# Banded attention and a cosine-gated layer on one core: the layer's tiles are moved between the attention heads, matmuls without use are added, and the PSUM pools become one

## The chip, the cores and the metric

The kernel runs on one core of a Trainium2 chip. The core has five engines that work through queues of their own, in order: TensorE (PE; its weight loads are listed as PEld), VectorE (DVE), ScalarE (ACT), GpSimd (POOL) and SyncE (SP), which here issues all DMAs. They wait for each other by semaphores. The metric is the time of one execution on the device in microseconds (us).

## What is computed

Eight batches of eight heads, 576 positions, head width 64. A query sees a key if they lie within 32 positions or if one of the two is among 8 global positions. The result, 4608 rows of 512, goes through a layer of width 2048 whose gate is `h * cos(h)`:

```
scores = q @ k.T / sqrt(64)
mask   = (abs(pos_i - pos_j) <= 32) | is_global_i | is_global_j
attn   = softmax(where(mask, scores, -1e9)) @ v     # 8 x 8 heads, 576 x 64
x      = attn, heads side by side                   # 4608 x 512
h      = x @ w_in                                   # 4608 x 2048
out    = (h * cos(h)) @ w_out                       # 4608 x 512
```

## The kernel before

**Start.** The mask is built once for five key blocks (`mask_sb`, five blocks of up to 128 keys by 576 queries; POOL writes a block in line 93). Both weight matrices are loaded and cast to float16 on ScalarE (lines 105 and 109).

**Attention, 64 heads.** Per head SyncE loads q, k and v in six DMAs; VectorE casts q and k, POOL casts v, which has an extra column of ones, so that the sum of the weights comes out beside the result. TensorE transposes q and k in five blocks each (line 148, tile `pst`), ScalarE copies them to `qT` and `kT` (line 149). For each of the five key blocks there are two score matmuls, of 512 and 64 queries (line 157, tile `ps`), two exps on ScalarE (line 163, to `e_sb`), and one multiply by the mask on VectorE (line 166, to `pmt`). For each of the five query blocks five matmuls over the key blocks follow (PV, line 175, tile `po`), a reciprocal (line 182), a scaling to `attn16` (line 184) and a DMA to `x_dram` in device memory (line 187).

**The layer, 36 tiles of 128 rows**, after all heads. Per tile: load the rows (line 203), four transposes (line 207) with ScalarE copies (line 208); for each of 16 column blocks four matmuls (line 213, `ph`), a cosine as a shifted sine on ScalarE (line 218), a multiply on VectorE (line 219, `gT`); then 16 matmuls of 512 columns (line 222, another tile named `po`), a copy (line 226) and a store (line 227).

**What sets the order.** The code is unrolled. A scheduler takes the instructions by their place in the code and by when it reckons their inputs and a free buffer to be there, and writes one fixed list for each engine; on the chip each list runs in order. The pools' buffer counts decide how far one step can run ahead of the next: in attention four buffers for transposes, two for scores, two for PV, two for `e_sb`, `recip` and `attn16`; in the layer two, four (`ph`) and two.

Of the kernel before, what the change touches and what calls it, by code (L numbers as in the profile page):

```python
# [18 lines left out]
def kernel(  # L19
# [56 lines left out]
    for kb in range(NKB):  # L76
        kbs = KBS[kb]
        pst = ps_small.tile([P, P], FP32, tag="isgt_ps")
# [3 lines left out]
    mask_sb = mpool.tile([P, NKB, S], FP16)  # L82
    for kb in range(NKB):
        kbs = KBS[kb]
# [15 lines left out]
    w_in16 = wpool.tile([P, DM // P, DFF], FP16)  # L100
    w_out16 = wpool.tile([P, DFF // P, DM], FP16)
# [9 lines left out]
    x_dram = dram.tile([NT, DM], FP16)  # L111

    qkv_pool = ctx.enter_context(tc.tile_pool(name="qkv", bufs=3))
    es_attn = ExitStack()
    tpsum = es_attn.enter_context(tc.tile_pool(name="tpsum", bufs=4, space=bass.MemoryType.PSUM))
    spsum = es_attn.enter_context(tc.tile_pool(name="spsum", bufs=2, space=bass.MemoryType.PSUM))
    opsum = es_attn.enter_context(tc.tile_pool(name="opsum", bufs=2, space=bass.MemoryType.PSUM))
    work = ctx.enter_context(tc.tile_pool(name="work", bufs=2))

    for b in range(B):  # L120
        for h in range(H):
            q_f32 = qkv_pool.tile([P, NKB, D], FP32, tag="qf32")
            k_f32 = qkv_pool.tile([P, NKB, D], FP32, tag="kf32")
# [11 lines left out]
            for kb in range(NKB):  # L135
                kbs = KBS[kb]
# [7 lines left out]
            for eng, src, dst in ((nc.scalar.copy, q_sb, qT), (nc.scalar.copy, k_sb, kT)):  # L144
                for kb in range(NKB):
                    kbs = KBS[kb]
                    pst = tpsum.tile([D, P], FP16, tag="tr")
                    nc.tensor.transpose(pst[:, :kbs], src[:kbs, kb], ident16[:kbs, :kbs])  # L148
                    eng(dst[:, kb * P : kb * P + kbs], pst[:, :kbs])  # L149

            pmt = work.tile([P, NKB, S], FP16, tag="pmt")
            for kb in range(NKB):
                kbs = KBS[kb]
                e_sb = work.tile([P, S], FP16, tag="e")
                for c0, cn in ((0, 512), (512, S - 512)):
                    ps = spsum.tile([P, 512], FP32, tag="st")
                    nc.tensor.matmul(  # L157
                        ps[:kbs, :cn],
                        kT[:, kb * P : kb * P + kbs],
                        qT[:, c0 : c0 + cn],  # L160
                        start=True, stop=True,
                    )
                    nc.scalar.activation(  # L163
                        e_sb[:kbs, c0 : c0 + cn], ps[:kbs, :cn], AF.Exp, scale=scale
                    )
                nc.vector.tensor_tensor(  # L166
                    pmt[:kbs, kb], e_sb[:kbs, :], mask_sb[:kbs, kb], ALU.mult
                )

            for qb in range(NKB):  # L170
                qbs = KBS[qb]
                po = opsum.tile([P, D + 1], FP32, tag="pv")
                for kb in range(NKB):
                    kbs = KBS[kb]
                    nc.tensor.matmul(  # L175
                        po[:qbs, :],
                        pmt[:kbs, kb, qb * P : qb * P + qbs],
                        v_sb[:kbs, kb, :],
                        start=(kb == 0), stop=(kb == NKB - 1),
                    )  # L180
# [11 lines left out]
    es_attn.close()  # L192

    xpool = ctx.enter_context(tc.tile_pool(name="xpool", bufs=2))
    xtpsum = ctx.enter_context(tc.tile_pool(name="xtpsum", bufs=2, space=bass.MemoryType.PSUM))
    hpsum = ctx.enter_context(tc.tile_pool(name="hpsum", bufs=4, space=bass.MemoryType.PSUM))
    outpsum = ctx.enter_context(tc.tile_pool(name="outpsum", bufs=2, space=bass.MemoryType.PSUM))
    NTT = NT // P
    NF = DFF // P
    NC = DM // P  # L200
    for t in range(NTT):
        x_sb = xpool.tile([P, DM], FP16, tag="x")
        nc.sync.dma_start(x_sb, x_dram[t * P : (t + 1) * P, :])
        xT = xpool.tile([P, NC, P], FP16, tag="xT")
        for j in range(NC):
            pst = xtpsum.tile([P, P], FP16, tag="xtr")
            nc.tensor.transpose(pst, x_sb[:, j * P : (j + 1) * P], ident16)
            nc.scalar.copy(xT[:, j], pst)  # L208
        gT = xpool.tile([P, NF, P], FP16, tag="gT")
        for f in range(NF):  # L210
            ph = hpsum.tile([P, P], FP32, tag="hT")
            for j in range(NC):
                nc.tensor.matmul(  # L213
                    ph, w_in16[:, j, f * P : (f + 1) * P], xT[:, j],
                    start=(j == 0), stop=(j == NC - 1),
                )
            cos_sb = xpool.tile([P, P], FP16, tag="cos")
            nc.scalar.activation(cos_sb, ph, AF.Sin, bias=pio2)  # L218
            nc.vector.tensor_tensor(gT[:, f], cos_sb, ph, ALU.mult)  # L219
        po = outpsum.tile([P, DM], FP32, tag="out")  # L220
        for f in range(NF):
            nc.tensor.matmul(  # L222
                po, gT[:, f], w_out16[:, f], start=(f == 0), stop=(f == NF - 1)
            )
        o_sb = xpool.tile([P, DM], FP32, tag="osb")
        nc.scalar.copy(o_sb, po)  # L226
        nc.sync.dma_start(out[t * P : (t + 1) * P, :], o_sb)


# [28 lines left out]
```

## Time and profile before

| | |
|---|---|
| median of six runs | 947.8 us (945.39 to 949.38) |
| the profiled execution | 945.39 us |
| its span, first to last instruction | 943.6 us |
| TensorE busy | 767.6 us (81%) |
| ScalarE busy | 564.4 us (60%) |
| VectorE busy | 470.3 us (50%) |
| POOL busy | 121.5 us (13%) |

Busy shares here are means over two stages that differ: attention up to about 613 us, the layer after it. A busy TensorE in this table is not TensorE at its peak, since matmuls overlap and their ends are modelled. A duration of one instruction contains its latency; what a row of them needs is read from the distance of their starts. "Waiting for" in a row names what came last, by semaphores.

### The profile page before, as it was taken

Reading aid. Unit: us, or ns where it says so; the run is one execution under the profiler, and the core shown is the slowest. Engines: PE = TensorE matmul, PEld = TensorE weight load, DVE = VectorE, ACT = ScalarE, POOL = GpSimd, SP = SyncE. Lnnn points to the kernel's source line nnn. Section 1 sums busy time; section 2 is a strip of 40 time slices with the busy share of each in tenths; the row PEclk is TensorE's granted clock in tenths of the full one; section 3 lists DMA queues with packets and bytes.
Section 4 is the critical chain, followed back from the end, with each engine's and each line's share of the span. In section 5 each row is a group of like instructions: output and inputs, shape, how many; then the busy total and the mean of one; then the engine's idle time right before and its main releaser. Section 6 shows DMA issues by size and latency. Waiting matters only on the chain.

```text
span 943.6 us, 19000 instructions
## 1 busy us (share of the span) xinstructions
PE 767.6 (81%) x5913; PEld 433.2 (46%) x5913; DVE 470.3 (50%) x1820; ACT 564.4 (60%) x2046; POOL 121.5 (13%) x406
## 2 busy tenths in 40 slices
PE   1688787777787887878878878799889889898997
PEld 0243333333343433434333344376666666666664
DVE  4454545444555455555555554455545445454453
ACT  3765555555455565555546556566766667667675
POOL 6211212121112112121121211100000000000000
PEclk9999999999999999999999999999999999999999
DMA  9433233332222322322222211010111111111110
GB/s 352 99 65 66 64 67 71 65 68 53 58 57 53 65 53 53 66 60 53 59 60 59 57 37 22 20 40 31 52 51 35 52 36 51 52 35 51 43 44 34
DMA packets 171798, 56.84 MB, mean 60 GB/s; under 512 B 159920, under 2 KB 164528, under 8 KB 171184
## 3 DMA queue, kind: packets, MB, share of 16 engines
q1 hardware_dynamic: 171696, 55.62, 23.5%
q8 instruction: 46, 0.75, 0.3%
q14 instruction: 56, 0.46, 0.2%
HBM read 41.42 MB, written 14.16 MB: 59 GB/s over the span
## 4 chain that ended last, share of the span: by engine, by line
PE 50%; ACT 21%; DVE 13%; issue 7%; DMA 7%; POOL 2%; ACTq 0%; SPq 0%; DVEq 0%; POOLq 0%
PE ps L157 14%; PE po L175 12%; ACT e_sb L163 11%; PE po L222 10%; PE ph L213 7%; DMA x_dram<-attn 7%; ACT cos_sb L218 6%; PE pst L148 6%; DVE gT L219 4%; DVE pmt L166 4%; ACT xT L208 2%; DVE attn L184 2%; POOL mask_sb L93 1%; DVE recip L182 1%; ACT w_out L109 1%
## 5 line engine op out<-in xcount | busy, mean ns | idle before, releaser
L163 ACT ACTIVATE e_sb<-ps 128x512 f16<-128x512 f32 (+3 forms) x640 | 230.3, 406 | 252.3 <-DVE pmt L166 158.0
L157 PE MATMUL ps<-qT,kT 64*128 64x512 f16 (+3 forms) x640 | 214.6, 424 | 88.8 <-ACT e_sb L163 79.4
L219 DVE TENSOR_TENSOR gT<-cos_sb,ph 128x128 f16<-128x128 f16 x576 | 157.5, 288 | 163.3 <-ACT cos_sb L218 162.5
L218 ACT ACTIVATE cos_sb<-ph,pio 128x128 f16<-128x128 f32 x576 | 182.1, 367 | 45.2 <-DVE gT L219 34.3
L213 PE MATMUL ph<-xT,w_in 128*128 128x128 f16 x2304 | 182.2, 219 | 29.8 <-DVE gT L219 15.8
L175 PE MATMUL po<-v_sb,pmt 128*128 128x65 f16 (+3 forms) x1600 | 181.2, 241 | 25.5 <-DVE attn L184 22.9
L213 PEld LDWEIGHTS <-w_in 128*128 128x128 f16 x2304 | 154.1, 97 | 72.4 <-issue 62.7
L175 PEld LDWEIGHTS <-pmt 128*128 128x128 f16 (+3 forms) x1600 | 117.2, 124 | 143.5 <-DVE attn L184 57.4
L166 DVE TENSOR_TENSOR pmt<-e_sb,mask_sb 128x576 f16<-128x576 f16 (+1 forms) x320 | 144.7, 459 | 60.7 <-ACT e_sb L163 59.5
L222 PE MATMUL po<-w_out,gT 128*128 128x512 f16 x576 | 152.6, 379 | 0.0
L182 DVE RECIPROCAL recip<-po 128x1 f32<-128x1 f32 (+1 forms) x320 | 52.6, 165 | 149.3 <-PE po L175 137.4
L157 PEld LDWEIGHTS <-kT 64*128 64x128 f16 (+1 forms) x640 | 62.6, 113 | 110.8 <-issue 100.7
L137 POOL CAST v_sb<-v_f 128x64 f16<-128x64 f32 (+1 forms) x320 | 101.4, 362 | 2.0 <-DMA v_f<-in_v_dram 2.0
L184 DVE TENSOR_SCALAR attn<-po,recip 128x64 f16<-128x64 f32 (+1 forms) x320 | 83.9, 274 | 32.0 <-DMA x_dram<-attn 30.8
L148 PE MATMUL pst<-ident,q_sb 128*64 128x128 f16 (+1 forms) x320 | 69.6, 302 | 22.4 <-DVE q_sb L139 17.0
L222 PEld LDWEIGHTS <-gT 128*128 128x128 f16 x576 | 53.4, 98 | 39.4
L134 POOL MEMSET v_sb<- 128x5 f16 x64 | 7.5, 119 | 467.8 <-PE po L175 446.4
L148 PE MATMUL pst<-ident,k_sb 128*64 128x128 f16 (+1 forms) x320 | 66.5, 302 | 0.0
L148 PEld LDWEIGHTS <-q_sb 128*64 128x64 f16 (+1 forms) x320 | 31.4, 136 | 76.2 <-issue 53.5
L149 ACT COPY kT<-pst 64x128 f16<-64x128 f16 (+1 forms) x320 | 62.3, 261 | 0.7 <-PE pst L148 0.7
L149 ACT COPY qT<-pst 64x128 f16<-64x128 f16 (+1 forms) x320 | 60.1, 253 | 0.0
L226 ACT COPY o_sb<-po 128x512 f32<-128x512 f32 x36 | 21.1, 585 | 59.1 <-PE po L222 59.1
(37 smaller groups left out, 213.5 us busy)
## 6 DMA issues: line engine op xcount, KB each, us to landing
out_dram<-o_sb SPq DMA_DIRECT2D x36, 256.0 KB, 2.2
q_f<-in_q_dram SPq DMA_DIRECT2D x64, 128.0 KB, 2.4
k_f<-in_k_dram SPq DMA_DIRECT2D x64, 128.0 KB, 2.4
v_f<-in_v_dram SPq DMA_DIRECT2D x64, 128.0 KB, 2.2
x_sb<-x_dram SPq DMA_DIRECT2D x36, 128.0 KB, 2.1
tmp_w<-in_moe_w_in_dram SPq DMA_DIRECT2D x1, 4096.0 KB, 12.4
tmp_w<-in_moe_w_out_dram SPq DMA_DIRECT2D x1, 4096.0 KB, 22.9
x_dram<-attn SPq DMA_DIRECT2D x256, 16.0 KB, 1.6
```

The lines of the kernel that those rows point to most:

```text
L137: nc.gpsimd.tensor_copy(v_sb[:kbs, kb, :D], v_f32[:kbs, kb])
L148: nc.tensor.transpose(pst[:, :kbs], src[:kbs, kb], ident16[:kbs, :kbs])
L149: eng(dst[:, kb * P : kb * P + kbs], pst[:, :kbs])
L157: nc.tensor.matmul(ps[:kbs, :cn], kT[:, kb * P : kb * P + kbs], qT[:, c0 : c0 + cn], start=True, stop=True,)
L163: nc.scalar.activation(e_sb[:kbs, c0 : c0 + cn], ps[:kbs, :cn], AF.Exp, scale=scale)
L166: nc.vector.tensor_tensor(pmt[:kbs, kb], e_sb[:kbs, :], mask_sb[:kbs, kb], ALU.mult)
L175: nc.tensor.matmul(po[:qbs, :], pmt[:kbs, kb, qb * P : qb * P + qbs], v_sb[:kbs, kb, :], start=(kb == 0), stop=(kb == NKB - 1),)
L184: nc.vector.tensor_scalar(attn16[:qbs], po[:qbs, :D], recip[:qbs, 0:1], None, ALU.mult)
L213: nc.tensor.matmul(ph, w_in16[:, j, f * P : (f + 1) * P], xT[:, j], start=(j == 0), stop=(j == NC - 1),)
L218: nc.scalar.activation(cos_sb, ph, AF.Sin, bias=pio2)
L219: nc.vector.tensor_tensor(gT[:, f], cos_sb, ph, ALU.mult)
L222: nc.tensor.matmul(po, gT[:, f], w_out16[:, f], start=(f == 0), stop=(f == NF - 1))
```

## The change

- A function `do_moe_tile(t)` holds the layer's tile, unchanged in its steps. In batches 2 to 8, after the second head, all tiles are computed whose rows come from batches before: four or five at a time, 31 in seven blocks. The last five follow after the last head.
- All PSUM tiles come from one pool of eight banks: `tr` (transposes of both stages) 2, `big` (scores, and the layer's output) 2, `sm` (PV, and `ph`) 3, `dummy` 1.
- Behind each score matmul of 512 queries stand three matmuls of 512 columns into `dummy`, which nobody reads: 15 per head, 960 in all. Their inputs are the identity and the first mask block.
- `recip` and `attn16` get eight buffers each in place of two.

```
-    tpsum = es_attn.enter_context(tc.tile_pool(name="tpsum", bufs=4, space=bass.MemoryType.PSUM))
-    spsum = es_attn.enter_context(tc.tile_pool(name="spsum", bufs=2, space=bass.MemoryType.PSUM))
-    opsum = es_attn.enter_context(tc.tile_pool(name="opsum", bufs=2, space=bass.MemoryType.PSUM))
+    psp = ctx.enter_context(tc.tile_pool(name="psp", bufs=1, space=bass.MemoryType.PSUM))
+    dummy = psp.tile([P, 512], FP32, tag="dummy")
...
+    def do_moe_tile(t):
+        x_sb = xpool.tile([P, DM], FP16, tag="x")
+        nc.sync.dma_start(x_sb, x_dram[t * P : (t + 1) * P, :])
+        xT = xpool.tile([P, NC, P], FP16, tag="xT")
+        for j in range(NC):
+            pst = psp.tile([P, P], FP16, tag="tr", bufs=2)
...
+            ph = psp.tile([P, P], FP32, tag="sm", bufs=3)
...
+        po = psp.tile([P, DM], FP32, tag="big", bufs=2)
...
+    ready_after = [((bb + 1) * S) // P for bb in range(B)]
+    moe_next = 0
...
+        avail = ready_after[b - 1] if b > 0 else 0
...
-                    pst = tpsum.tile([D, P], FP16, tag="tr")
+                    pst = psp.tile([D, P], FP16, tag="tr", bufs=2)
...
-                    ps = spsum.tile([P, 512], FP32, tag="st")
+                    sps = psp.tile([P, 512], FP32, tag="big", bufs=2)
...
+                    if cn == 512:
+                        for _ in range(3):
+                            nc.tensor.matmul(dummy, ident16, mask_sb[:, 0, :512], start=True, stop=True)
...
-                po = opsum.tile([P, D + 1], FP32, tag="pv")
+                pvt = psp.tile([P, P], FP32, tag="sm", bufs=3)
+                po = pvt[:, : D + 1]
...
-                recip = work.tile([P, 1], FP32, tag="recip")
+                recip = work.tile([P, 1], FP32, tag="recip", bufs=8)
...
-                attn16 = work.tile([P, D], FP16, tag="attn16")
+                attn16 = work.tile([P, D], FP16, tag="attn16", bufs=8)
...
+            if b > 0:
+                target = avail if h == 1 else 0
+                while moe_next < target:
+                    do_moe_tile(moe_next)
+                    moe_next += 1
+
+    while moe_next < NTT:
+        do_moe_tile(moe_next)
+        moe_next += 1
```

The order moves with it. The dummies depend on nothing but the first mask block, so the scheduler puts them wherever it reckons a gap: 64 in a row before the first transpose, 28 more after the second, nine in each steady head, the others around the blocks of tiles. TensorE's list in a steady head before (`ps` are scores, `pst` transposes, `po` PV; numbers tell tiles apart); five PV matmuls of one query block stand together, and only once all five of the head's masked blocks are there:

```order
L157 MATMUL ps_4154<-qT_4112,kT_4113 128x512
L157 LDWEIGHTS kT_4113
L157 MATMUL ps_4157<-qT_4112,kT_4113 128x64
L148 LDWEIGHTS k_sb_4243
L148 MATMUL pst_4285<-ident16_68,k_sb_4243 64x128
L148 LDWEIGHTS k_sb_4243
L148 MATMUL pst_4288<-ident16_68,k_sb_4243 64x128
L148 LDWEIGHTS k_sb_4243
L148 MATMUL pst_4291<-ident16_68,k_sb_4243 64x64
L175 LDWEIGHTS pmt_3844
L175 MATMUL po_3907<-v_sb_3794,pmt_3844 128x65
```

The same engine in a steady head of the changed kernel (`sps` are scores, `pvt` PV):

```order
L200 LDWEIGHTS ident16_68
L200 MATMUL dummy_187<-mask_sb_113,ident16_68 128x512
L192 LDWEIGHTS kT_3177
L192 MATMUL sps_3243<-qT_3176,kT_3177 128x512
L192 LDWEIGHTS kT_3177
L192 MATMUL sps_3249<-qT_3176,kT_3177 128x64
L214 LDWEIGHTS pmt_3208
L214 MATMUL pvt_3264<-v_sb_3158,pmt_3208 128x65
L214 LDWEIGHTS pmt_3208
L214 MATMUL pvt_3275<-v_sb_3158,pmt_3208 128x65
```

A dummy stands between the scores, and PV now takes the key blocks as they come, for three query blocks at a time.

ScalarE's list in the second and third head of a batch before (exps and the copies of `qT`, `kT`):

```order
L163 ACTIVATE e_sb<-ps 128x512
L163 ACTIVATE e_sb<-ps 128x64
L163 ACTIVATE e_sb<-ps 64x512
L163 ACTIVATE e_sb<-ps 64x64
L149 COPY qT<-pst 64x128 x3
L163 ACTIVATE e_sb<-ps 128x512
```

and after, at the start of a block of tiles (`xT`, `cos_sb` and `o_sb` belong to the layer):

```order
L201 ACTIVATE e_sb<-sps 64x512
L201 ACTIVATE e_sb<-sps 64x64
L130 COPY xT<-pst 128x128 x3
L140 ACT_TABLE_LOAD
L140 ACTIVATE cos_sb<-ph,pio_70 128x128 x16
L130 COPY xT<-pst 128x128 x2
L148 COPY o_sb<-po 128x512
```

and at its end:

```order
L140 ACTIVATE cos_sb<-ph,pio_70 128x128 x14
L148 COPY o_sb<-po 128x512
L184 COPY qT<-pst 64x128 x2
L184 COPY qT<-pst 64x64
L184 COPY kT<-pst 64x128 x3
L201 ACT_TABLE_LOAD
L201 ACTIVATE e_sb<-sps 128x512
```

No exp stands between the cosines of a block, and each block has a table load at either end: 16 loads in the list, where before there are 2.

## Rows read from the trace of the kernel before

**Rows 1.** The page: TensorE busy and clock granted, tenths in 40 slices.
```profile
PE   1688787777787887878878878799889889898997
PEclk9999999999999999999999999999999999999999
```
**Rows 2.** Windows: start:end, length, busy us (x instructions) by engine, clock, DMA.
```profile
core 0: us, PE busy (x) PEld busy (x) DVE busy (x) ACT busy (x) POOL busy (x), PEclk, DMA share, GB/s
40.00:600.00 560.00, 449.20 (x2752) 217.17 (x2752) 284.90 (x1155) 313.28 (x1239) 99.52 (x360) 1.00 0.27 57
640.00:936.00 296.00, 266.93 (x2753) 184.80 (x2751) 143.18 (x526) 201.04 (x686) 0.00 (x0) 1.00 0.13 44
```
**Rows 3.** Groups by line and form: count, busy us, mean ns, idle before.
```profile
L222 PE MATMUL po<-w_out,gT 128*128 128x512 f16 x576 | 152.6, 379 | 0.0
L157 PE MATMUL ps<-qT,kT 64*128 64x512 f16 x256 | 151.6, 592 | 66.4 <-ACT e_sb L163 57.4
```
**Rows 4.** Timeline of TensorE at the stages' border: start us, us, what.
```profile
613.28 1.33 PE L213 MATMUL ph<-xT,w_in 128*128 128x128 f16 x11 [0.23 <-ACT e_sb L163]
614.41 0.59 PE L175 MATMUL po<-v_sb,pmt 128*128 128x65 f16 x5
614.93 0.71 PE L213 MATMUL ph<-xT,w_in 128*128 128x128 f16 x5
...
618.65 0.42 PE L175 MATMUL po<-v_sb,pmt 128*128 128x65 f16 x5
619.00 1.30 PE L213 MATMUL ph<-xT,w_in 128*128 128x128 f16 x16
```
**Rows 5.** Chain that ended last: whole span, then the window 296 to 314 us.
```profile
PE ps L157 14%; PE po L175 12%; ACT e_sb L163 11%; PE po L222 10%; PE ph L213 7%; DMA x_dram<-attn 7%; ACT cos_sb L218 6%; PE pst L148 6%; DVE gT L219 4%; DVE pmt L166 4%; ACT xT L208 2%; DVE attn L184 2%; POOL mask_sb L93 1%; DVE recip L182 1%; ACT w_out L109 1%
...
by line: PE ps L157 25.6%; PE po L175 22.7%; DMA x_dram<-attn 19.2%; ACT e_sb L163 16.5%; PE pst L148 9.9%; issue 6.3%; DVE attn L184 3.2%; DVE pmt L166 2.2%; DVE recip L182 1.3%; ACTq L163 0.1%
```
**Rows 6.** Timeline of TensorE in one head.
```profile
300.70 0.67 PE L157 MATMUL ps<-qT,kT 64*128 64x512 f16 x2
301.30 0.42 PE L148 MATMUL pst<-ident,q_sb 128*64 128x128 f16 x2
301.51 0.62 PE L175 MATMUL po<-v_sb,pmt 128*64 128x65 f16 x5
```
**Rows 7.** The page's DMA issues: count, KB each, median us to landing.
```profile
x_sb<-x_dram SPq DMA_DIRECT2D x36, 128.0 KB, 2.1
...
x_dram<-attn SPq DMA_DIRECT2D x256, 16.0 KB, 1.6
```
**Rows 8.** Timeline of SyncE's queue, first and last of a dense stretch.
```profile
248.82 0.38 SPq L129 DMA_DIRECT2D v_f<-in_v_dram  x1
...
255.80 0.80 SPq L187 DMA_DIRECT2D x_dram<-attn  x2
```
**Rows 9.** Layer: pieces of the chain (first two), then TensorE's timeline.
```profile
640.08 2.37 PE po L222 x11
...
937.48 2.39 PE po L222 x11
...
720.58 2.54 PE L222 MATMUL po<-w_out,gT 128*128 128x512 f16 x11
```
**Rows 10.** Timelines of the start and of the switch, all engines.
```profile
8.03 2.21 POOL L93 TENSOR_SCALAR mask_sb<-band,isg_cols 128x576 f16<-128x576 f32 x1 [2.31 <-DVE isg_cols L80]
...
31.82 0.84 ACT L149 COPY qT<-pst 64x128 f16<-64x128 f16 x5
...
33.10 0.66 PE L157 MATMUL ps<-qT,kT 64*128 64x512 f16 x2
...
35.15 0.29 PE L175 MATMUL po<-v_sb,pmt 128*128 128x65 f16 x2
...
612.53 0.70 ACT L163 ACTIVATE e_sb<-ps 64x512 f16<-64x512 f32 x2 [0.49 <-DVE pmt L166]
613.97 1.28 ACT L218 ACT_TABLE_LOAD   x1 [0.74 <-PE ph L213]
615.26 0.62 ACT L218 ACTIVATE cos_sb<-ph,pio 128x128 f16<-128x128 f32 x2
```

More of the change, by code (lines that the diff above doesn't have):

```diff
@@ L113 @@
     qkv_pool = ctx.enter_context(tc.tile_pool(name="qkv", bufs=3))
-    es_attn = ExitStack()
-    tpsum = es_attn.enter_context(tc.tile_pool(name="tpsum", bufs=4, space=bass.MemoryType.PSUM))
-    spsum = es_attn.enter_context(tc.tile_pool(name="spsum", bufs=2, space=bass.MemoryType.PSUM))
-    opsum = es_attn.enter_context(tc.tile_pool(name="opsum", bufs=2, space=bass.MemoryType.PSUM))
+    psp = ctx.enter_context(tc.tile_pool(name="psp", bufs=1, space=bass.MemoryType.PSUM))
     work = ctx.enter_context(tc.tile_pool(name="work", bufs=2))
+    xpool = ctx.enter_context(tc.tile_pool(name="xpool", bufs=2))
+    dummy = psp.tile([P, 512], FP32, tag="dummy")
+    NTT = NT // P
+    NF = DFF // P
+    NC = DM // P
+    def do_moe_tile(t):
[4 more added lines that the diff above has]
+            pst = psp.tile([P, P], FP16, tag="tr", bufs=2)
+            nc.tensor.transpose(pst, x_sb[:, j * P : (j + 1) * P], ident16)
+            nc.scalar.copy(xT[:, j], pst)
+        gT = xpool.tile([P, NF, P], FP16, tag="gT")
+        for f in range(NF):
+            ph = psp.tile([P, P], FP32, tag="sm", bufs=3)
+            for j in range(NC):
+                nc.tensor.matmul(
+                    ph, w_in16[:, j, f * P : (f + 1) * P], xT[:, j],
+                    start=(j == 0), stop=(j == NC - 1),
+                )
+            cos_sb = xpool.tile([P, P], FP16, tag="cos")
+            nc.scalar.activation(cos_sb, ph, AF.Sin, bias=pio2)
+            nc.vector.tensor_tensor(gT[:, f], cos_sb, ph, ALU.mult)
+        po = psp.tile([P, DM], FP32, tag="big", bufs=2)
+        for f in range(NF):
+            nc.tensor.matmul(
+                po, gT[:, f], w_out16[:, f], start=(f == 0), stop=(f == NF - 1)
+            )
+        o_sb = xpool.tile([P, DM], FP32, tag="osb")
+        nc.scalar.copy(o_sb, po)
+        nc.sync.dma_start(out[t * P : (t + 1) * P, :], o_sb)
+    ready_after = [((bb + 1) * S) // P for bb in range(B)]
+    moe_next = 0
     for b in range(B):
+        avail = ready_after[b - 1] if b > 0 else 0
         for h in range(H):
@@ L155 @@
                 for c0, cn in ((0, 512), (512, S - 512)):
-                    ps = spsum.tile([P, 512], FP32, tag="st")
+                    sps = psp.tile([P, 512], FP32, tag="big", bufs=2)
                     nc.tensor.matmul(
-                        ps[:kbs, :cn],
+                        sps[:kbs, :cn],
                         kT[:, kb * P : kb * P + kbs],
@@ L162 @@
                     )
+                    if cn == 512:
+                        for _ in range(3):
+                            nc.tensor.matmul(dummy, ident16, mask_sb[:, 0, :512], start=True, stop=True)
                     nc.scalar.activation(
-                        e_sb[:kbs, c0 : c0 + cn], ps[:kbs, :cn], AF.Exp, scale=scale
+                        e_sb[:kbs, c0 : c0 + cn], sps[:kbs, :cn], AF.Exp, scale=scale
                     )
@@ L190 @@
                 )
[L192 to L227, printed above, removed]
+            if b > 0:
[6 more added lines that the diff above has]
+        moe_next += 1
 _INS = ['q', 'k', 'v', 'global_idx', 'moe_w_in', 'moe_w_out']
```

## The prediction

> **What bounds the kernel now.** I read the two stages apart, because they have different limits. The page's slices show TensorE at seven to eight tenths up to about 600 us and at nine tenths after that, and its clock row shows the full level throughout [rows 1]. The windows give the same: 449.20 of 560 us in attention, 266.93 of 296 us in the feed-forward stage, with ScalarE at 313.28 and VectorE at 284.90 of 560, so that no engine is full in attention [rows 2].
>
> Is the clock row right? The same 512 columns take 592 ns in attention (score matmul, L157) and 379 ns in the feed-forward stage (L222) [rows 3]. The change can be seen on one line: five PV matmuls take 0.59 us at 614.41 and 0.42 us at 618.65, in the same shapes; from 613.28 on TensorE had begun to run `ph` matmuls densely between them [rows 4]. So I take attention as run at the lower level (1.2 GHz) and the rest at the upper (2.4 GHz), against the clock row. The Trainium skill (TensorE: Matmul & The Clock Gate, Single matmul latency) gives (219+512)/1.2 = 609 ns and (398+512)/2.4 = 379 ns, as estimates; and its part on the clock gate warns that the recorded throttle events are unreliable. If the clock row were right instead, the gain by the level below would fall away; that is the third rival.
>
> In attention the end is set by a chain and not by an engine. Its steady state, two heads long: scores 25.6%, PV 22.7%, the landing of `x_dram` stores 19.2%, exp 16.5%, transposes 9.9%, all else 12.7% [rows 5]. Of 18.0 us that is 4.6, 4.1, 3.46, 2.97, 1.78 and 2.3. The landing stands there because `attn16` has two buffers: VectorE, in order, waits for a store and holds back the mask multiply behind it, for which exp waits. Over the run the landings are 7% of the chain, 66 us [rows 5]. One head takes (613.23 - 33.10)/64 = 9.06 us [rows 10]. A feed-forward tile takes (937.48 - 640.08)/33 = 9.01 us [rows 9].
>
> **The buffers.** `attn16` and `recip` go from 2 to 8. A store lands in 1.6 us in the median [rows 7]; eight buffers are 1.6 heads, some 10 us. The wait goes: -1.73 us per head. What is next late there is the PV group itself.
>
> **The dummies.** 960 matmuls of 512 columns. Eleven in a row take 2.54 us with one tail of 0.379, so 0.216 us each at the upper level [rows 3, 9]. The order puts 92 ahead of the third transpose and nine into each steady head, the rest around the switches. The first 64 need the first mask slice, written by 8.03 + 2.21 = 10.24 us [rows 10]. At the lower level (twice 0.216) for some 16 and then the upper, they end at 10.24 + 6.9 + 10.4 = 27.5; two transposes and 28 more end at 33.8, while ScalarE is busy with the weights until 31.82 [rows 10]. The transposes after them, that stood done before, come late: +3 us at the start (between 0 and 20, the latter if all 92 run at the lower level).
>
> In a steady head they are worth the level. Lower level: a score pair 0.60 us, two transposes 0.21 [rows 6], a PV group 614.93 - 614.41 = 0.52; upper: 619.00 - 618.65 = 0.35 [rows 4], a factor of 0.67, which I use for all three. Chain: 18.0 - 3.46 (stores) - 0.33 x 10.5 (TensorE's parts) = 11.1 us for two heads, 5.5 per head. The dummies cost 9 x 0.216 = 1.94 us of TensorE per head. TensorE holds 7.0 of those 11.1 us, so at most 1.2 of it lies on the chain unless the chain turns to TensorE altogether; I take 1.2: 6.7 us.
>
> This has to stand above what each queue needs per head:
> - TensorE at the upper level: 5 x 0.40 + 5 x 0.35 + 5 x 0.14 + 1.94 = 6.4 us (at half instead of 0.67 for scores and transposes, 5.7).
> - SyncE: eleven DMAs. Fourteen in a dense stretch took 255.80 + 0.80 - 248.82 = 7.78 us, 0.556 each, so 6.1 us [rows 8]. It was hidden under 9.06 us and is now close to the bound; loads run up to three heads ahead, which covers single waits but not the rate.
> - ScalarE 313.28 x 9.06/560 = 5.1 us, VectorE 4.6 us [rows 2].
>
> So 6.7 us per head, with 6.1 (SyncE's floor) and 8.0 (6.1 and all the dummies in line) as bounds. 64 heads: 429 us (390 to 512), for 580 before.
>
> **PSUM.** One pool: transposes 4 to 2 buffers, PV 2 to 3 and `ph` 4 to 3 in one tag, scores and `po` two in one tag. In a head ScalarE copies two transposes between two exps, so two buffers meet the order. For a tile, a `ph` buffer comes free after four matmuls, cosine, multiply, some 1.3 us; three buffers give one per 0.43 us, while a tile needs one per 9.01/16 = 0.56. I take 9.1 us per tile, 36 x 9.1 = 328 us (324 to 340).
>
> **The feed-forward tiles moved forward.** 31 of 36 go into seven blocks. By the order nearly nothing of attention runs inside a block: it is a drain, four or five tiles and a refill, so I book no overlap as gain. Each block adds a refill (first copies at 31.82 to first PV at 35.15, 3.3 us), a table load of 1.28 us with exp queued behind it, and a drain: the last masks, PV, reciprocals and PV again, by the same rows about 2.5 us [rows 10]. The second load, cosine's, lies under that drain. 7 x 7.1 = 50 us; with half of it hidden 25, with the tables' second load and the dummies inside a block in line 70. The Trainium skill (ScalarE: Activation LUTs, What ACT_TABLE_LOAD costs) adds about 1380 ns of drain to each 1283 ns load; with its figure the 14 added loads would make the sum some 19 us longer, as an estimate. The trace shows 1.28 us, then the first cosine at once, after an idle 0.74 us whose end is a matmul's [rows 10]. At the very end the first tile must wait for the last head's first rows to be stored and read back: 1.6 + 2.1 us and two issues, +5 us [rows 7], where it was ready before.
>
> **Sum.** Before: 33.1 + 64 x 9.06 + 36 x 9.01 = 937.3, and the span is 943.6, so 6 us at the ends. After: 33.1 + 3 + 429 + 328 + 50 + 5 + 6 = 854 us of span. The profiled execution's time is 945.39, 1.8 over its span, and the median of the six runs is 2.4 us over that: 854 + 4 = 858.
>
> **Rivals.**
> 1. *The lower level stays in attention.* Then a head needs 5 x 0.60 + 5 x 0.52 + 5 x 0.21 + 9 x 0.43 = 10.5 us of TensorE and the dummies are the bound: 33 + 20 + 672 + 328 + 50 + 5 + 6 = 1114 us. It is slower from 8.1 us per head on ((943.6 - 33 - 3 - 328 - 50 - 5 - 6)/64). For it: attention ran 580 us with TensorE busy for 80% and never rose. Against: `ph` matmuls raised it within about 4 us [rows 4], the 64 leading dummies are as dense, and it never fell over 36 tiles with short waits in each. The Trainium skill (same page, HAM oscillation) says that idle stretches between bursts bring the level down again; no row here shows one long enough to try it, and the drains at the seven switches would be the place. 10%.
> 2. *Dummies in line.* They have no waits of their own and stand ahead of scores and PV in an in-order queue; if every one is on the path a head takes 8.0 us: 33 + 3 + 512 + 328 + 50 + 5 + 6 + 4 = 941. For it: TensorE's own 6.4 us is the highest floor. Against: PV now follows its masks by two steps, which leaves it slack. Heads of 7.4 to 8.1 us, 900 to 945: 17%, of it 3% within 0.2% of 947.8.
> 3. *The level was never low* and 592 ns is another cost of scores. A head: 9.0 - 1.73 + 1.2 = 8.5 us, 973 us. The PV rows speak against it, since they differ in the same shape. 3%.
> 4. *Everything hides*: heads at 6.1, switches at 25 us: 429 - 390 = 39 and 25 less, 794. 10%.
> That the change overlaps the two stages, as it is arranged to, I take as not happening; it is in the forecast at nothing.
>
> **How the numbers follow.** The forecast, 800 to 900, has 60%. A measurement of this kernel tells 0.2% from no change. Faster: 60 + 10 + 14 = 84%; same 3%; slower 13%. For 8 in 10 the range takes the forecast and most of rivals 2 and 4, the bounds 6.1 and 8.0 of the head: 797 to 940.
>
> **What would show it.** In the trace of the changed kernel: score matmuls of 512 columns near 380 ns, not 592, from the first head on (level); no wait of VectorE for `x_dram` stores; a steady head of 6.7 us between the same instructions of two heads; SyncE nearly without gaps there; nine dummies 0.216 us apart when back to back; tiles at 9.1 us; seven gaps of some 7 us between the last exp of a head and the first PV after a block, less the tiles. Score matmuls near 600 ns in any stretch would make it wrong, and so would heads above 8 us, or exp waiting longer than 1 us for masks.

## The result, and the profile after

The changed kernel takes 876.58 us (median of 8 runs, 876.23 to 877.85), the kernel before 947.58 us beside it (median of 16, 944.65 to 950.52): a ratio of 0.9255, with a 95% interval of 0.9243 to 0.9267. The forecast was 858, in a range of 797 to 940. The profiled execution has a span of 874.8 us, where 854 was summed. One execution of a kernel of the next section (all dummies, tiles last) took 1257.23 us, with a mean granted clock of 0.553 over its whole span, against 913.56 to 915.11 us in its other three, and stands in no number below.

The page, TensorE's busy tenths and granted clock in 40 slices, and the chain by line (answering to [rows 1] and [rows 5]):

```profile
PE   6999999999999999999999999999999999999697
PEclk9999999999999999999999999999999999999799
...
PE dummy L200 28%; PE ph L135 14%; PE sps L192 14%; PE po L144 13%; PE pvt L214 11%; PE pst L183 10%; ACT cos_sb L140 2%; DVE gT L141 1%; PE pst L129 1%; ACT xT L130 1%; SPq L164 0%; DMA q_f<-in_q_dram 0%; POOL mask_sb L93 0%; DMA x_sb<-x_dram 0%; SPq L168 0%
```

The landing of the stores, 7% of the chain in [rows 5], is gone. TensorE stands in its place, with the dummy matmuls as the largest entry. The same in windows (columns as in [rows 2]: start:end, length, busy us by engine, clock), one in the steady attention and one at the last head's end:

```profile
260.00:310.00 50.00, 50.00 (x358) 23.96 (x356) 27.19 (x119) 36.00 (x136) 7.48 (x36) 1.00 0.24 49
805.00:833.00 28.00, 21.08 (x176) 12.72 (x175) 11.75 (x48) 15.39 (x49) 0.00 (x0) 0.82 0.10 23
```

In attention TensorE is busy 50.00 of 50 us, where it was 449.20 of 560; every other engine has room. The wide score and the dummy, by form (count, busy us, mean ns, idle before), answer to [rows 3], where a wide score took 592 ns:

```profile
L192 PE MATMUL sps<-qT,kT 64*128 64x512 f16 x256 | 98.9, 386 | 0.0
L200 PE MATMUL dummy<-mask_sb,ident 128*128 128x512 f16 x960 | 306.1, 386 | 1.7 <-DVE isg_cols L80 1.7
```

So the upper level holds in all of the attention up to its last head. TensorE's timeline over one head, from a score pair to the same pair of the next head:

```profile
280.16 0.42 PE L192 MATMUL sps<-qT,kT 64*128 64x512 f16 x2
...
280.74 0.21 PE L183 MATMUL pst<-ident,q_sb 64*64 64x64 f16 x1
280.88 0.24 PE L183 MATMUL pst<-ident,k_sb 128*64 128x128 f16 x1
281.05 0.39 PE L200 MATMUL dummy<-mask_sb,ident 128*128 128x512 f16 x1
...
282.27 0.39 PE L200 MATMUL dummy<-mask_sb,ident 128*128 128x512 f16 x1
282.50 0.26 PE L214 MATMUL pvt<-v_sb,pmt 128*128 128x65 f16 x3
282.59 0.38 PE L200 MATMUL dummy<-mask_sb,ident 128*128 128x512 f16 x1
282.90 0.39 PE L192 MATMUL sps<-qT,kT 64*128 64x512 f16 x1
283.22 0.24 PE L183 MATMUL pst<-ident,k_sb 128*64 128x128 f16 x1
...
287.44 0.42 PE L192 MATMUL sps<-qT,kT 64*128 64x512 f16 x2
```

A head takes 287.44 - 280.16 = 7.28 us, where 6.7 was forecast. Counted from each start to the next, its nine dummies take 2.58 us of it, the scores 1.94, the transposes 1.33 and PV 1.43. The last eight matmuls of a tile's output, one row at the same place of three batches (blocks of five and of four tiles lie between them):

```profile
220.97 1.89 PE L144 MATMUL po<-w_out,gT 128*128 128x512 f16 x8
...
328.52 1.89 PE L144 MATMUL po<-w_out,gT 128*128 128x512 f16 x8
...
427.16 1.89 PE L144 MATMUL po<-w_out,gT 128*128 128x512 f16 x8
```

The two distances, 107.55 and 98.64 us, differ by one tile: 8.91 us. What is left of the shorter one, 98.64 - 4 x 8.91 - 8 x 7.28 = 4.8 us, is the price of a block, with the dummies that stand in it. The tail, TensorE's timeline:

```profile
818.14 0.82 PE L214 MATMUL pvt<-v_sb,pmt 128*128 128x65 f16 x10 [0.52 <-DVE attn L223]
823.03 0.39 PE L129 MATMUL pst<-ident,x_sb 128*128 128x128 f16 x2 [4.07 <-DMA x_sb<-x_dram]
...
827.32 1.06 PE L144 MATMUL po<-w_out,gT 128*128 128x512 f16 x2
```

TensorE waits 4.07 us for the last head's rows to come back. Two `po` matmuls then take 1.06 us, where [rows 9] has eleven in 2.54: this is the window with a clock of 0.82, and the only fall of the level that this kernel's clock row shows.

### The profile page after: what moved, and what is told of

The parts are those of the page before. It is cut to its first block, busy times and chain, and to the rows that moved or that the text cites. A ratio compares the mean times of both kernels' runs of the same rounds, so it can differ in the third digit from the quotient of the medians.

```text
span 874.8 us, 20658 instructions
## 1 busy us (share of the span) xinstructions
PE 850.9 (97%) x6873; PEld 465.1 (53%) x6873; DVE 455.9 (52%) x1820; ACT 614.0 (70%) x2060; POOL 95.2 (11%) x406
## 4 chain that ended last, share of the span: by engine, by line
PE 91%; ACT 3%; DVE 2%; SPq 1%; issue 1%; DMA 1%; POOL 0%; ACTq 0%; DVEq 0%
PE dummy L200 28%; PE ph L135 14%; PE sps L192 14%; PE po L144 13%; PE pvt L214 11%; PE pst L183 10%; ACT cos_sb L140 2%; DVE gT L141 1%; PE pst L129 1%; ACT xT L130 1%; SPq L164 0%; DMA q_f<-in_q_dram 0%; POOL mask_sb L93 0%; DMA x_sb<-x_dram 0%; SPq L168 0%
## 5 line engine op out<-in xcount | busy, mean ns | idle before, releaser
L201 ACT ACTIVATE e_sb<-sps 128x512 f16<-128x512 f32 (+3 forms) x640 | 239.0, 406 | 117.3 <-PE sps L192 114.4
L200 PE MATMUL dummy<-mask_sb,ident 128*128 128x512 f16 x960 | 306.1, 386 | 1.7 <-DVE isg_cols L80 1.7
L140 ACT ACTIVATE cos_sb<-ph,pio 128x128 f16<-128x128 f32 x576 | 203.1, 368 | 40.1 <-PE ph L135 18.0
L192 PE MATMUL sps<-qT,kT 64*128 64x512 f16 (+3 forms) x640 | 153.5, 290 | 0.2 <-ACT e_sb L201 0.2
L214 PE MATMUL pvt<-v_sb,pmt 128*128 128x65 f16 (+3 forms) x1600 | 146.9, 197 | 1.5 <-DVE pmt L204 1.0
L214 PEld LDWEIGHTS <-pmt 128*128 128x128 f16 (+3 forms) x1600 | 99.2, 99 | 78.2 <-issue 17.2
L200 PEld LDWEIGHTS <-ident 128*128 128x128 f16 x960 | 85.2, 97 | 62.8 <-issue 9.7
L221 DVE RECIPROCAL recip<-pvt 128x1 f32<-128x1 f32 (+1 forms) x320 | 39.7, 157 | 78.9 <-PE pvt L214 54.4
L172 POOL CAST v_sb<-v_f 128x64 f16<-128x64 f32 (+1 forms) x320 | 74.8, 278 | 35.8 <-DMA v_f<-in_v_dram 35.5
L223 DVE TENSOR_SCALAR attn<-pvt,recip 128x64 f16<-128x64 f32 (+1 forms) x320 | 76.2, 274 | 0.7 <-DVE k_sb L175 0.2
```

The lines of the kernel that those rows point to most:

```text
L192: nc.tensor.matmul(sps[:kbs, :cn], kT[:, kb * P : kb * P + kbs], qT[:, c0 : c0 + cn], start=True, stop=True,)
L200: nc.tensor.matmul(dummy, ident16, mask_sb[:, 0, :512], start=True, stop=True)
L201: nc.scalar.activation(e_sb[:kbs, c0 : c0 + cn], sps[:kbs, :cn], AF.Exp, scale=scale)
L214: nc.tensor.matmul(po[:qbs, :], pmt[:kbs, kb, qb * P : qb * P + qbs], v_sb[:kbs, kb, :], start=(kb == 0), stop=(kb == NKB - 1),)
L223: nc.vector.tensor_scalar(attn16[:qbs], po[:qbs, :D], recip[:qbs, 0:1], None, ALU.mult)
```

## The experiments

Twelve kernels were run, each beside the kernel before, which took 944.3 to 944.5 us (medians) in these sets and 947.6 in the set of the result; so a difference between times of two sets is good to some 3 us. The first eight ask what the dummies, the buffers and the place of the tiles are worth alone; the last four why the place of the tiles matters.

### Without the dummies

```diff
-                    if cn == 512:
-                        for _ in range(3):
-                            nc.tensor.matmul(dummy, ident16, mask_sb[:, 0, :512], start=True, stop=True)
```

> The changed kernel without its 960 dummies, all else left. Theory A (the dummies hold TensorE at the upper level and are worth more than they cost): the score matmuls of 512 columns go back to about 592 ns in attention, a head takes 7.3 to 8.0 us by TensorE's content at the lower level (6.65 us) and the chain without store waits, and the kernel 890 to 930 us, slower than 877. Theory B (the level, once raised, stays by itself; the tiles between the heads raise it): 592 ns only up to the first block of tiles, then 380 ns; heads of about 6.0 us after it; 805 to 840 us. Theory C (the level has no part; the dummies only cost): 380 ns throughout, 800 us.

Measured: 888.69 us, ratio 0.9411 (0.9397 to 0.9425). The page's clock row, two windows, the wide score in the first of them, and the same transpose of two heads (all of this kernel):

```profile
PEclk9999999655995559855797557955599555965599
...
180.00:200.00 20.00, 19.98 (x120) 9.55 (x119) 11.40 (x53) 13.35 (x53) 3.26 (x16) 0.50 0.19 38
240.00:260.00 20.00, 18.16 (x192) 12.72 (x191) 10.35 (x37) 15.22 (x48) 0.00 (x0) 1.00 0.11 41
...
L192 PE MATMUL sps<-qT,kT 64*128 64x512 f16 x11 | 6.6, 599 | 0.0
...
184.12 0.26 PE L183 MATMUL pst<-ident,q_sb 64*64 64x64 f16 x1
...
191.87 0.26 PE L183 MATMUL pst<-ident,q_sb 64*64 64x64 f16 x1
```

Attention is at 0.50 (1.2 GHz), the blocks of tiles at 1.00 (2.4 GHz), and a wide score takes 599 ns at the lower level, as it did before (592). A head takes 7.75 us with TensorE full. The dummies thus do what they are for, and are worth only 12 us (15 by the two ratios). In a dense head the gain is 7.75 - 7.28 = 0.47 us: counted from each start to the next, the upper level takes the head's own matmuls from 7.75 us to 7.28 - 2.58 = 4.70, and the nine dummies take 2.58 of the 3.05 us gained. Not all of 64 x 0.47 = 30 us arrives. Between the same score matmul of the first and the last head, the intervals without a block are 22 us shorter in all than in this kernel; the seven with a block, in each of which 43 to 48 dummies stand, are 8 us longer, and the first head's comes 2 us later.

### The leading dummies alone

```diff
+    for _ in range(92):
+        nc.tensor.matmul(dummy, ident16, mask_sb[:, 0, :512], start=True, stop=True)
 ...
-                        for _ in range(3):
-                            nc.tensor.matmul(dummy, ident16, mask_sb[:, 0, :512], start=True, stop=True)
```

> The changed kernel without the dummies at the scores, but with 92 in a row before the first head, in the start's idle time. Theory A: upper level in the first head, then a fall within a few heads, time as without dummies, 890 to 930 us. Theory B: upper level from the first head to the end, heads of about 6.0 us, 795 to 815 us. The difference to the run without any is 0 for A and about 15 us for B (ten heads at 1.6 us).

Measured: 890.0 us, ratio 0.9432 (0.9416 to 0.9448). The clock row:

```profile
PEclk9855569655995559855797557955599555965599
```

The level is up when the first head begins and gone from 40 us on (0.50 in the window from 40 to 60 us). It does not stay by itself.

### One dummy behind each wide score

```diff
-                        for _ in range(3):
+                        for _ in range(1):
```

> The changed kernel with one dummy per key block in place of three, 320 in all. The scheduler puts them early: 92 at the start, nine per head, and the last of them stand in the third batch; after that no head has one. Theory A: 380 ns up to the third batch, 592 ns in the heads after it, except right behind a block of tiles; 880 to 920 us. Theory B: 380 ns throughout, heads of 7.3 us with dummies and 6.0 us without, 815 to 835 us.

Measured: 883.81 us, ratio 0.9362 (0.9348 to 0.9376). The clock row:

```profile
PEclk9999999999995559755797558955599555965599
```

The dummies have no inputs that they wait for, so the order places them at any gap of an earlier head: 224 of the 320 run between 35 and 212 us, at the density of the changed kernel. There the level holds; without them it goes in the next attention stretch, and theory A is right.

### Eight buffers alone

```diff
-                recip = work.tile([P, 1], FP32, tag="recip")
+                recip = work.tile([P, 1], FP32, tag="recip", bufs=8)
 ...
-                attn16 = work.tile([P, D], FP16, tag="attn16")
+                attn16 = work.tile([P, D], FP16, tag="attn16", bufs=8)
```

> The kernel before with eight buffers for recip and attn16 in place of two, and nothing else. The store landings were 7% of its chain, 66 us, and 19% in a steady stretch, 1.73 us per head. If that time goes off the chain, the kernel takes 837 (1.73 x 64) to 882 us (66) and no wait of VectorE for x_dram stores is left. If the next wait is just as late (TensorE at the lower level, exp waiting for masks), it takes 930 to 948 us. Score matmuls stay at 592 ns either way.

Measured: 967.28 us, ratio 1.0245 (1.023 to 1.0261): slower. The stores' landings have left the chain, as forecast, and yet a head takes 9.6 us and not 9.06. Both expectations missed. The timeline of SyncE's queue, and the longest of the engines' waits (engine, line, what it waited for: us in total, times, longest) over 100 to 600 us:

```profile
305.45 0.59 SPq L129 DMA_DIRECT2D q_f<-in_q_dram  x1
308.19 3.80 SPq L187 DMA_DIRECT2D x_dram<-attn  x5
312.04 0.59 SPq L133 DMA_DIRECT2D q_f<-in_q_dram  x1
312.68 0.58 SPq L129 DMA_DIRECT2D k_f<-in_k_dram  x1
...
POOL v_sb L137 <- DMA v_f<-in_v_dram: 266.7, 53, 6.9
```

After 306.04 the queue stands still until five stores may go at 308.19; the second half of one load and all of K's loads are behind them, though nothing holds these loads but their place in the queue. GpSimd waits 266.7 us for V's loads. That wait is not on the chain, which from 300 to 319 us is scores, PV, exp, transposes and short steps of VectorE and holds no DMA. What did change is the order: 51 heads of this kernel have one and the same list of TensorE matmuls, and no head of the kernel before has that list. The queue's row suggested the last four runs.

### No dummies, tiles last

The first kernel of this section with `target = 0` in place of `target = avail if h == 1 else 0`: all 36 tiles after the last head.

> The changed kernel without dummies and with all 36 tiles after the last head, as in the kernel before: what is left of the change is the PSUM split (PV 3 buffers, transposes 2) and the eight buffers. If the blocks of tiles cost refills and table loads as predicted (7.1 us each), it takes 33 + 64 x 7.75 + 36 x 9.0 + 12 = 865 us, 24 below the run with tiles between the heads. If moving the tiles costs nothing or gains, 885 to 900 us. Either way well under 944, where the buffers alone gave 967: that would put the gain on the third PV buffer.

Measured: 955.11 us, ratio 1.0102 (1.008 to 1.0124), 66 us more than with the tiles between the heads and against both expectations. Its window of steady attention, TensorE's timeline there, and the chain from 300 to 319 us:

```profile
110.00:590.00 480.00, 391.45 (x2295) 185.17 (x2294) 232.79 (x966) 270.67 (x1021) 59.71 (x305) 1.00 0.27 56
...
303.43 0.64 PE L192 MATMUL sps<-qT,kT 64*64 64x512 f16 x2 [0.35 <-ACT e_sb L198]
...
305.29 0.34 PE L211 MATMUL pvt<-v_sb,pmt 64*128 64x65 f16 x3 [0.63 <-DVE pmt L201]
...
306.96 1.11 PE L211 MATMUL pvt<-v_sb,pmt 128*128 128x65 f16 x10
...
by line: PE sps L192 34.6%; PE pvt L211 22.4%; ACT e_sb L198 17.0%; PE pst L183 16.4%; DVE pmt L201 4.9%; issue 3.1%; ACT kT L184 2.8%; DVE recip L218 1.6%; DVE attn L220 1.0%
```

Until the head that ends at 105 us its heads last as long as those of the kernel with blocks, to 0.02 us: 7.7 us, then 11.1, 9.4, 8.6, 8.7. There the other kernel comes to its first block and goes on with 7.75; this one stays at 10.24 and 8.67 in turn, 9.45 us. TensorE's work is the same (391.45/480 x 9.45 = 7.71 us); 1.7 us of idle time a head has come in, between bursts of ten and more PV matmuls. No load stands on the chain. The blocks hid nothing. They changed the heads behind them.

### Five dummies a head that wait for their head

In the kernel without dummies, one dummy behind each key block's mask multiply, with the masked weights as its stationary operand, so that it can't run ahead; first with the tiles between the heads, then with the tiles last.

```diff
+                for _ in range(1):
+                    nc.tensor.matmul(dummy, pmt[:kbs, kb, :P], mask_sb[:kbs, 0, :512], start=True, stop=True)
```

> The changed kernel with one dummy per key block, five per head, 320 in all, whose weights are the masked block pmt of that key block (first 128 queries), so that the scheduler cannot run them ahead: they spread evenly over all heads. If five per head hold the upper level: 380 ns for the scores throughout, heads of 6.0 to 6.5 us, 790 to 815 us. If they do not: 592 ns in attention, five dummies at 0.43 us on a full TensorE, heads of 8.2 to 9.8 us, 910 to 1010 us.

> The same with all tiles after the last head. If five hold the level: 33 + 64 x 6.3 + 324 + 12 = 772 us, lower by the cost of seven blocks than with tiles between. If they do not: 900 us or more, and no tile stage raises the level before the end of attention.

Measured: 1004.45 us, ratio 1.0628 (1.0599 to 1.0657), and 1040.55 us, ratio 1.101 (1.0986 to 1.1035). A window of the first, and the dummy by form in the second (110 to 690 us):

```profile
180.00:200.00 20.00, 20.00 (x108) 8.71 (x105) 8.72 (x39) 10.74 (x43) 2.64 (x12) 0.50 0.22 46
...
L205 PE MATMUL dummy<-mask_sb,pmt 128*128 128x512 f16 x216 | 131.3, 608 | 9.1 <-DVE pmt L201 7.2
```

Five dummies in every head run at the lower level and do not raise it, in the first kernel not even where a block of tiles had just raised it: the level goes while the next head starts, where TensorE is idle for up to 1.49 us, and does not come back before the next block. They are pure cost: the first rival of the prediction, at five dummies instead of nine.

### All dummies, tiles last

The changed kernel with `target = 0`.

> The changed kernel with its 960 dummies and all tiles after the last head. The dummies that stood in and around the blocks go into the heads: (960 - 92)/64 = 13.6 per head in place of nine. If each costs its time on a full TensorE: heads of 7.28 + 4.6 x 0.22 = 8.3 us, 34.7 + 531 + 324 + 8 = 898 us. If the blocks cost more than that, 850 to 877 us.

Measured: 915 us, ratio 0.9674 (0.9648 to 0.9699), above both expectations. With dummies too the tiles between the heads are worth 38 us.

### Stores on another queue, no dummies, tiles last

```diff
-                nc.sync.dma_start(
+                nc.gpsimd.dma_start(
                     x_dram[b * S + qb * P : b * S + qb * P + qbs, h * D : (h + 1) * D],
```

> All 36 tiles stand after the last head, there is no dummy matmul, and the five attention stores of a head are issued from GpSimd's queue and not from SyncE's; everything else is as in the changed kernel. Asked is why taking the tiles between the heads gave 66 us without dummies (955.1 against 888.7 us) although TensorE's work in a head is the same: a head lasts 7.75 us with TensorE always busy between the blocks, and 10.24 and 8.67 us in turn, 9.45 on average, with 1.6 us of idle TensorE, where no block comes. Theory, the queue: on SyncE's queue the six loads of a later head stand in order behind five stores that wait for attention results, so after five heads the loads are late and the list of TensorE's instructions is laid out in bursts of ten to sixteen PV matmuls; a block of tiles lets the loads catch up. With the stores on another queue the dense order holds for all heads without any block: start 33, 64 heads x 7.75 = 496, 8 for the last head's PV, 332 for the tiles: about 869 (855 to 885), lower level in the attention. Rival, the block itself: the heads gain by work of the tiles that lies beside them, and the queue does not matter: 955, within 10. Second rival: the stores cost GpSimd more than they cost SyncE, and its copies of V come late: above 955.

Measured: 858.54 us (858.4 to 859.3), ratio 0.909 (0.9073 to 0.9106). Steady attention in a window, the same transpose of two heads, and GpSimd's issues by line:

```profile
110.00:500.00 390.00, 389.73 (x2266) 184.84 (x2265) 216.68 (x958) 259.47 (x1008) 190.12 (x552) 1.00 0.30 67
...
299.64 0.26 PE L183 MATMUL pst<-ident,q_sb 64*64 64x64 f16 x1
...
307.39 0.26 PE L183 MATMUL pst<-ident,q_sb 64*64 64x64 f16 x1
...
L223 POOL DMA_DIRECT2D x_dram<-attn x320 | 173.9, 546 | 258.3 <-DVE attn L220 241.1
```

The queue is the cause. One edit on the kernel of 955 us, where the rival said that the queue does not matter, takes 97 us off: 7.75 us a head from the eighth to the last (7.7 in the three before), TensorE 389.73 of 390 us busy, and no block needed. It beats the changed kernel without a dummy and without a tile moved. Against the first kernel of this section, which has the same heads and seven blocks, it is 888.7 - 858.5 = 30 us faster: 4.3 us for each block.

The traces also say how the queue acts. 56 heads of this kernel have one and the same list of TensorE matmuls. In the kernel with tiles between the heads and the stores on SyncE's queue, 26 heads behind the blocks have exactly this list, and they too take 7.75 us; in the kernel of 955 us no head has it. Under the same list the queue made no difference. So the 97 us come with the order that the scheduler wrote when the loads no longer stood behind stores; that late loads hold the engines up on the chip is not shown.

### The same with 640 dummies

```diff
+                        for _ in range(2):
+                            nc.tensor.matmul(dummy, ident16, mask_sb[:, 0, :512], start=True, stop=True)
```

> As the kernel before this one, with dummy matmuls of 512 columns: two behind each wide score, 640 in all, of which TensorE's list holds nine in each head from the second to the sixtieth; the tiles stand after the last head. Theory: with the dense order and the level held, a head takes 7.28 us, as in the changed kernel between its blocks, no block has to be entered or left, and the tiles take 332 us: start 35, 64 x 7.28 = 466, 8, 332: about 841 (830 to 860), faster than the changed kernel. Rival: dummies and order do not add up, because the blocks of tiles are what brings the level back each time and nine dummies in a head only keep it for a while: the level falls somewhere in the attention and stays low, each head then takes 7.75 plus nine dummies at the lower level (nine times 0.43), 11.6 us, up to 1115 us, and the time depends on where it falls. Second rival, no effect of the queue: 915, as with 960 dummies, the tiles last and the stores on SyncE.

Measured: 832.81 us (832.54 to 833.07), ratio 0.8815 (0.8796 to 0.8833): the fastest of all, 44 us under the changed kernel. Its clock row, two windows, and TensorE's timeline where the level falls (the first row is the last dummy):

```profile
PEclk9999999999999999999999957999999999999999
...
300.00:400.00 100.00, 100.00 (x747) 48.34 (x746) 61.75 (x261) 70.99 (x274) 52.25 (x148) 1.00 0.32 72
480.00:500.00 20.00, 19.81 (x119) 9.29 (x117) 10.00 (x44) 13.61 (x53) 9.05 (x21) 0.50 0.05 11
...
473.70 0.39 PE L200 MATMUL dummy<-mask_sb,ident 128*128 128x512 f16 x1
...
475.69 0.42 PE L192 MATMUL sps<-qT,kT 64*128 64x512 f16 x2
...
476.77 0.54 PE L192 MATMUL sps<-qT,kT 64*128 64x512 f16 x2
```

7.28 us a head with nine dummies in each, as in the changed kernel. From the sixty-first head on they are used up: those heads take 7.7 us, and the clock falls to 0.50 there, until the tiles bring it back. It falls with TensorE busy: 19.96 of the 20 us from 460 to 480.

### Before's PSUM, eight buffers, stores on GpSimd

The kernel of the fourth experiment with the queue's edit.

> The kernel before with two of the edits: eight buffers instead of two for the reciprocal and the attention tile, and a head's five stores issued from GpSimd's queue. PSUM is split as before (four transpose buffers, two for scores, two for PV; no dummies; tiles last). Asked is whether the new split of PSUM has a part in the dense heads. Eight buffers alone were slower (967.3 us, heads of 9.6 us, SyncE's queue late). Theory, the queue is all: with the stores off SyncE's queue TensorE is always busy here too, 7.75 us a head at the lower level, about 860 us (850 to 875), as with the new split (858.5). Rival, the split: with two PV buffers, and four transposes standing in a row, TensorE still waits for the masks and the copies, heads of about 8.5 to 9.1 us, 905 to 945 us.

Measured: 894.7 us, ratio 0.9466 (0.9452 to 0.9481). A window, and the wait in each head:

```profile
200.00:300.00 100.00, 95.05 (x541) 45.96 (x540) 53.84 (x229) 61.71 (x240) 51.47 (x133) 1.00 0.28 63
...
305.68 0.64 PE L157 MATMUL ps<-qT,kT 64*128 64x512 f16 x2 [0.36 <-ACT e_sb L163]
```

Between the two expectations: 8.34 us a head. Against the kernel before beside each, the queue turns the buffers' +23 us into -50. The rest to 858.5, 36 us or 0.59 us a head, is what the new split of PSUM gives (three PV buffers for two, two for transposes): no other edit of the attention is left between the two kernels.

### Five dummies that wait, in the dense order

Stores on GpSimd's queue, tiles last, and one dummy a key block that reads the masked weights as its moving operand (`nc.tensor.matmul(dummy, ident16[:kbs], pmt[:kbs, kb, :512], start=True, stop=True)`).

> Stores on GpSimd's queue and tiles after the last head, as in the two kernels before, with five dummies of 512 columns in every head, one behind each key block's masked weights, which it reads as its moving operand, so that it can't be placed ahead of its head. Asked is whether five of them hold the upper level once TensorE has no idle time; five such dummies in the heads with idle time did not (1040.5 us). Theory A, the idle time brought the level down there: the level stays, a head takes 7.28 less four dummies of 0.22, 6.4 us, at least what VectorE and ScalarE need (5.6 us busy), 35 + 64 x 6.4 + 340 = 785 (775 to 815). Theory B, five dummies are too few also without idle time: lower level in the attention, a head takes 7.75 plus five of 0.43, 9.9 us: 35 + 634 + 340 = 1009 (985 to 1040).

Measured: 990.38 us, ratio 1.0484 (1.0466 to 1.0501). A window and the dummy by form (110 to 640 us):

```profile
200.00:300.00 100.00, 100.00 (x513) 42.87 (x511) 43.84 (x196) 54.21 (x207) 40.70 (x111) 1.00 0.24 54
...
L205 PE MATMUL dummy<-pmt,ident 128*128 128x512 f16 x216 | 131.2, 607 | 0.0
```

TensorE has no idle time at all, and the dummies still run at 607 ns, the lower level. So it was not the idle time that kept the level down with five dummies a head. The clock row shows 1.00 in this window because it shows full until the first change on record; the durations decide.

## Why the prediction came out as it did

The sum that holds, in steps of one edit up to the fifth row, and again from the sixth (head: us between the same instructions of steady heads):

| kernel | us | head |
|---|---|---|
| before | 947.6 | 9.06 |
| eight buffers | 967.3 | 9.6 |
| and the stores on GpSimd's queue | 894.7 | 8.34 |
| and the new split of PSUM | 858.5 | 7.75 |
| and 640 dummies | 832.8 | 7.28 |
| buffers and split, stores on SyncE, tiles last | 955.1 | 9.45 |
| with the tiles between the heads | 888.7 | 7.75 |
| and 960 dummies: the changed kernel | 876.6 | 7.28 |

**Level: right.** Attention before ran at 1.2 GHz against its clock row. The kernel without dummies shows the same durations with the clock of 0.50 on record, and the changed one 386 ns. The third rival falls.

**Buffers: wrong as a step of its own.** The wait went, as said; the 1.73 us a head did not come. "What is next late there is the PV group itself" is the sentence that failed: with eight buffers the head took 9.6 us, in another order of instructions, and 8.34 once the loads no longer stood behind stores that wait for results. SyncE's queue was in the prediction as a rate (6.1 us a head, under 9.06) and with three heads of loads ahead. The rate was no limit; the order in the queue was, through the list that the scheduler made of it.

**Dummies: right on the level, wrong on the path.** Nine a head, and the level held. But the chain of 5.5 us with 1.2 of dummies on it did not come: TensorE is full, and all nine are in line. The step that failed is "at most 1.2 of it lies on the chain unless the chain turns to TensorE altogether": it did turn. That is the second rival's mechanism; its 8.0 us came from SyncE's 6.1 beside the dummies, where TensorE's own 4.70 stand. TensorE's floor was in the prediction, at 6.4 us with the dummies, 0.9 short. Against its terms, by the starts in the head above: dummies 2.58 for 1.94, ten transposes 1.33 for 0.7, scores 1.94 for 2.0, PV 1.43 for 1.75. A dummy holds back the PV matmuls behind it, which read 128 rows like itself, for 0.23 us (282.27 to 282.50), near the 0.216 used. Where the next matmul's rows change from 128 to 64, it is 0.31 to 0.33 us (282.59 to 282.90); six of the nine dummies stand so. A wide score, of 64 rows, holds back the next one of 128 rows as long (282.90 to 283.22). A transpose, taken at 0.07 us from one pair in a row, takes 0.14 and 0.17 at 280.74 and 280.88.

**Tiles moved: right on overlap, wrong on the sum.** No overlap was booked, and none came. A block cost 4.8 us by the periods and, without dummies, 4.3 by the difference of two kernels, where 7.1 was taken. But moving them gave 66 us without dummies (38 with them), because the heads behind a block got the dense order that the stores on SyncE's queue otherwise prevent. Nothing in the prediction had this. A kernel without the dummies and with only the tiles moved would have been forecast slower.

**So the time was near for a mixture of reasons.** Against the forecast's 854 us of span: heads 64 x 0.58 = 37 more, blocks 7 x 2.3 = 16 less, tiles 36 x 0.19 = 7 less, the start 1 less (first score at 34.72 us). What is left of 874.8 us by this count is 20 us, where 11 were taken; in it are the ends, the slow stretch of the tail, and 5 us of longer heads before the first block. What the prediction took for two gains, buffers and level, was one gain of the order, by the blocks and the new split of PSUM, and a small one of the level. That errors of both signs met near the forecast was luck.

**Start, tiles, tail.** 34.7 for 36.1; 8.91 for 9.1 us. The idle 4.07 us in the tail is the +5 of the forecast; what it lacked is the level that the idle time costs. The Trainium skill (TensorE: Matmul & The Clock Gate, HAM oscillation) says that idle stretches between bursts bring the level down. The prediction found no row long enough; this one agrees (4.07 us idle, then 0.82). But the kernel with 640 dummies lost the level with TensorE busy for 19.96 of 20 us, and the last one with five dummies stayed low at 100 of 100: idle stretches are not its only cause.

**The table loads.** The page ScalarE: Activation LUTs of the Trainium skill (What ACT_TABLE_LOAD costs) gives about 1380 ns of drain for each load. ScalarE's timeline of the changed kernel at a block's end does not show it:

```profile
358.39 0.42 ACT L184 COPY kT<-pst 64x128 f16<-64x128 f16 x2 [0.45 <-PE pst L183]
358.82 1.28 ACT L201 ACT_TABLE_LOAD   x1
360.12 0.60 ACT L201 ACTIVATE e_sb<-sps 128x512 f16<-128x512 f32 x1
```

The load begins 0.01 us after the copy ends, and exp 0.02 us after the load.

**Open.** Nine dummies a head hold a level that stands, and five do not raise it, in heads that are equally full. Whether five would hold it, had it stood when the full heads began, was not tried: in the kernel with blocks idle time comes between. What the chip goes by, no run here shows. A tile held back from the last block, so that it lies under the 4.07 us of the tail, was not tried. Why the scheduler writes the one order or the other was not followed further than to the queue that issues the stores.

## What to carry to other kernels

Ask of each in-order queue not only how much it carries but who stands behind whom: loads that wait for nothing, queued behind stores that wait for results, cost the dense order of a whole stage here, and one word (the queue that issues the stores) was worth 97 us, where the whole change gave 71. Before filler work is put in to hold a clock level, compare the time of the work at either level with the filler's own: here it gave 3.05 us a head and took 2.58. And when a change gains, take each part away alone; one of this one's parts (eight buffers) lost time by itself, and its largest gain (the order behind the blocks) was a side effect.

## What the runs showed of the hardware

- The clock row shows the full level until the first change on record: the kernel without dummies has 1.00 from 45 to 100 us and 0.50 from 180 to 200 us, at equal durations (592 and 599 ns for a wide score).
- The lower level was granted over stretches in which TensorE was hardly ever idle (0.50 at 19.98 of 20 us without dummies, and 607 ns dummies at 100.00 of 100), and the level fell in one (19.96 of 20 us).
- GpSimd takes 546 ns (mean of 320) to issue a store of 16 KB or less, as long as SyncE takes for one of its DMAs (0.556 us) [rows 8], and had the room: in steady attention it is busy 190 of 390 us in all.
- At the upper level a matmul of 512 columns holds back the next one by 0.216 us in a row of its kind, by 0.23 before others of the same rows, and by 0.31 to 0.33 where the operand's rows change from 128 to 64 or back.
